# A two-block kernel on one core: every second transfer of K~ moves to SP's queue, and the fallback flag is loaded inside the order

## The chip, the cores and the metric

The kernel runs on one core of one Trainium2 chip. The metric is the device time of one execution in microseconds (us); a lower number is better. A core has five engines that run their own instruction streams: PE (TensorE, matmuls), DVE (VectorE), ACT (ScalarE), POOL (GpSimd) and SP (SyncE). PE, DVE and ACT do most of the computing; SP only issues transfers; ACT and POOL issue some too. Engines wait for each other, and for transfers, on semaphores.

## The reference

The inputs are q, k, v, a_re and a_im of shape (4, 8, 768, 48), w_in (384 x 2048) and w_out (2048 x 384), all float32. The first block is a gated linear recurrence per batch and head, the second a dense block with a squared ReLU:

```
a = (a_re + i a_im) * min(|a|, 0.999) / (|a| + 1e-6)
for t in range(768):
    S = a[t][:, None] * S + outer(k[t], v[t])     # S complex, 48 x 48
    y[t] = q[t] @ real(S)
x = y, heads side by side                         # 3072 x 384
out = relu(x @ w_in)**2 @ w_out                   # 3072 x 384
```

## The kernel before, in words

The 3072 tokens are cut into six **units** of L = 512 (n = 0 to 5, `NU` = 6). A unit has eight heads in four pairs (`NP` = 4); z = 0 and 1 are the two halves of the heads, each with two pairs (p or q_ = 0 and 1). A sequence is 768 long, so units 1 and 4 hold the end of one sequence and the beginning of the next, and units 2 and 5 hold the end of one.

For each unit, `load` brings a, q, k and v; `chain` normalises a and forms cumulative products of it (mostly DVE and ACT); `apply` inside it multiplies q and k by these products or their inverses, which gives Q~ and K~ in the tiles `ff` (the products at line 1326, K~ first). A token's place in `ff` is partition by partition with four tokens each. `gather` (line 1351) is called as soon as K~ is there: it moves K~ by DMA into `KC`, where a block i of 128 tokens (i = 0 to 3) lies on the partitions. `needs(n)` lists the blocks that are wanted: [0, 1, 2, 3] for units 0 and 3, [0, 2, 3] for 1 and 4, [0, 1, 2] for 2 and 5. `places(i)` gives one transfer for an even block and two of 64 partitions each for an odd one. In units 0 to 2 (`FINE`) a gather covers one pair (np = 1), in the later ones two.

Then come the steps of `pairs` for each pair: `turn` transposes Q~ and K~ to `QT` (DVE transposes at line 1414 and twelve transfers at line 1419, SP and ACT; some pairs by PE instead), `score` (line 1461) multiplies them, `keep` (line 1489) reads `KC` to update the state, `mix` (lines 1520 and 1524) forms y, and transfers at line 1546 (mostly SP) put y into `xT`. The dense block of the unit reads `xT`: `dense` (line 1571, then line 1619 or, for units 1 to 5, `seven` with matmuls at line 1682 in the helper `half`), and for the last unit `eleven` (line 1827) ahead of `seven`. Its outputs leave by `rows` (line 1637, POOL) or, for the last group, `side` (line 1631, SP and one by ACT). DVE's adds for it are at line 1707, its sums of activations (`put`) at line 1698.

The order of all of this isn't the order of the code. Every call of `step` or `dma` only adds an entry to a `Plan` with an engine, an estimated duration, the keys that it reads and writes, a rank and the function that issues it. `Plan.order` (line 524) is a list scheduler over the engines SP, POOL, PE, DVE and ACT: it repeatedly takes the engine that can go first and the best-ranked entry that is ready there. A transfer costs the issuing engine 0.55 us (POOL) or 0.6 us (SP, ACT), takes its turn on a common bus and lands a given time later; of POOL's transfers, and of SP's and ACT's together, at most eight are in flight. PE gets 0.3 us of margin behind another engine's result, or 1.7 us for `score` and `keep` behind a transfer, and 0.12 us for each turn between small matmuls (`score`, `mix`) and others. `Plan.emit` (line 614) then issues the functions in the planned order of their starts. So each engine's stream is in planned order, and what runs is held together by semaphores.

The fast path is valid for inputs in a certain range. `inspect` and `verdict` check that beside the last matmuls: DVE writes 0 or 1 into the one-element tile `flag` (line 1893, behind a one-column matmul at line 1891). After the fast path, `nc.values_load` (line 1958) loads the flag into a register of every engine, and `tc.If(bad > 0)` (line 1959) branches past or into `general_path`. For these inputs the branch skips the general path.

Lines 1637 (`rows`), 888 (`inspect`), 844 (`fetch`) and 949 (values v) are POOL's other transfers; lines 933 (`load`), 1419, 1546 and 1631 are SP's.

Of the kernel before, what the change touches and what calls it, by code (L numbers as in the profile page):

```python
# [481 lines left out]
class Plan:  # L482
# [5 lines left out]
    RATE = 280e3  # L488
    LANES, LANDED = 8, 0.2
    STOP, COLD = 2.4, 3.5  # L490
    TURN = 0.12
    SETTLED, GROUP = 90.0, 6
    HOLD, URGENT, FILL = {"DVE": 0.15, "ACT": 0.8}, (2, 0.2), (2, 0.2)
# [30 lines left out]
    def order(self):  # L524
# [14 lines left out]
        def small(n):  # L539
            return any(x in steps[n][3].__qualname__ for x in ("score", "mix"))  # L540
# [20 lines left out]
        while len(start) < len(steps):  # L561
# [30 lines left out]
            if e == "PE":  # L592
                if small(n) != tiled:
                    dur, tiled = dur + self.TURN, small(n)
                if t > free[e] + self.STOP:
# [15 lines left out]
        self.start, self.done = start, done  # L611
        return sorted(start, key=lambda n: (start[n], n))

    def emit(self):
        for n in self.order():
            self.steps[n][3]()


U16, I16, F16 = mybir.dt.uint16, mybir.dt.int16, mybir.dt.float16
# [3 lines left out]
def fast_path(ctx, tc, q, k, v, a_re, a_im, moe_w_in, moe_w_out, out, flag):  # L623
# [4 lines left out]
    nc = tc.nc  # L628
# [20 lines left out]
    EARLY = 2  # L649
# [12 lines left out]
    dve, pool, act, sp = nc.vector, nc.gpsimd, nc.scalar, nc.sync  # L662
# [88 lines left out]
    plan = Plan()  # L751
# [30 lines left out]
    def kk_(z, qs=(0, 1), js=range(W)):  # L782
        return [("KC", z, q_, j) for q_ in qs for j in js]

    def fk(z, *qs, ps=(0, 1)):
        return [("f", z, q_, p) for q_ in qs for p in ps]

    def dma(q, reads, writes, fn, rank, size, lat=1.8, group=None):
        name, dur = ("POOL", 0.55) if q is pool else ("SP" if q is sp else "ACT", 0.6)
        step(name, dur, reads, writes, fn, rank, (lat, size), group)  # L790
# [119 lines left out]
    def places(i):  # L910
        return [(CH, 0, CH), (0, CH, CH)] if i % 2 else [(0, 0, C)]
# [41 lines left out]
    def chain(n):  # L953
# [284 lines left out]
        def apply(z, p, np):  # L1238
# [81 lines left out]
            for j in (1, 0):  # L1320
                o = own[:, j * nh * W * R:(j + 1) * nh * W * R].rearrange(
                    "p (c h e) -> p h c e", c=W, h=nh)
                for r in range(2):
                    step("DVE", tt(n1), [("a", z), ("ap", z, p, r)] + held[r] + (kf[0] + x("kk") if j else [("qk", z)]),
                         kf[j],
                         lambda j=j, r=r, o=o: dve.tensor_tensor(  # L1326
                             out=o[:, :, :, r * D:(r + 1) * D], in0=kk if j else qk[:, 0],
                             in1=al[r], op=ALU.mult), rk)
                if j:
                    gather(n, z, p, np)  # L1330
# [11 lines left out]
    def needs(n):  # L1342

        ps_ = parts(n)
        ends = ps_[-1][3] + ps_[-1][1] * W == S
        got = [0, 1, 2] + ([] if ends else [3])
        if len(ps_) > 1:
            got.remove(1)
        return got

    def gather(n, z, p, np):
        rank = (PAIR, n)
        w = 2 * np * R
        kc = KC[z].rearrange("p (i x) -> p i x", i=W)[:, :, p * 2 * R:p * 2 * R + w]
        nat = ff[z][:, p * Z:(p + np) * Z].rearrange("p (j c x) -> p j c x", j=2, c=W)[:, 1]
        keys = fk(z, *range(2 * p + np, 2 * p + 2 * np))
        for i in needs(n):
            for p0, t0, m in places(i):
                queue = sp if n < EARLY and i % 2 else pool
                src = nat[32 * i + t0 // W:32 * i + (t0 + m) // W]  # L1360
                dma(queue, keys, kk_(z, range(p, p + np), [i]),
                    lambda i=i, p0=p0, m=m, src=src, queue=queue: queue.dma_start(  # L1362
                        out=kc[p0:p0 + m, i], in_=src),
                    rank, m * w * NEAR, GLAT, group=(n, p))
# [568 lines left out]
        inspect(i)  # L1933
    verdict()
    with tc.manual_schedule():
        plan.emit()


@with_exitstack
def kernel(  # L1940
    ctx: ExitStack,
    tc: tile.TileContext,
    q: bass.AP,
    k: bass.AP,
    v: bass.AP,
    a_re: bass.AP,
    a_im: bass.AP,
    moe_w_in: bass.AP,
    moe_w_out: bass.AP,
    out: bass.AP,  # L1950
):

    nc = tc.nc
    fp = ctx.enter_context(tc.tile_pool(name="flag", bufs=1))
    flag = fp.tile([1, 1], I32, name="flag")
    args = (q, k, v, a_re, a_im, moe_w_in, moe_w_out, out)
    fast_path(tc, *args, flag)
    bad = nc.values_load(flag[0:1, 0:1], min_val=0, max_val=1)
    with tc.If(bad > 0):
        general_path(tc, *args)  # L1960

# [29 lines left out]
```

## Time and profile before

| | |
|---|---|
| median of three runs | 663.11 us (662.74 to 663.75) |
| the profiled execution | 663.12 us |
| its span, first to last instruction | 661.2 us |
| mean granted clock of TensorE | 0.990 |
| DMA packets, bytes | 55268, 80.35 MB |

The profile is one execution, recorded on the chip. Its page gives the busy time of each engine, the span in 40 slices (16.5 us each; a digit is the busy share in tenths), the chain of work that ended last, and the costliest groups of instructions by source line. Further views can be asked of the trace: who waited for whom, the stretches with each engine's busy time, the instructions of one line, the timeline of one engine. PEld is the loading of weights into PE. A letter q behind an engine (SPq, ACTq) means its sequencer: an instruction that issues, waits or branches. An issue of a DMA shows only the time to issue it; the landing is listed apart. A duration written as three numbers is least, median and most in ns.

### The profile page before, as it was taken

To read this page: it belongs to the slowest core of one execution; us is meant where nothing else is said; L and a number is where in the kernel's file an instruction comes from. 1 tells how busy PE (TensorE), PEld (TensorE's weight loads), DVE (VectorE), ACT (ScalarE), POOL (GpSimd) and SP (SyncE) were. 2 spreads that over 40 slices of the span, in tenths; PEclk is the share of its full clock that TensorE was granted. 3 is DMA by queue.
4 is the path that set the end of the run, shared out by engine and by line. 5 is a ranking of instruction groups with operands and counts; after the bars stand their busy time and mean duration, and the time that the engine had idled before them with its cause. 6 is when DMAs were issued, how large, how long until landed. Compare 5 with 4: busy or idle time off the path is not lost.

```text
span 661.2 us, 12107 instructions
## 1 busy us (share of the span) xinstructions
PE 620.8 (94%) x4454; PEld 555.5 (84%) x4454; DVE 583.9 (88%) x1191; ACT 347.0 (52%) x606; POOL 118.7 (18%) x198
## 2 busy tenths in 40 slices
PE   0378999999999999999999999999999999999996
PEld 0357887687779988999989989989999989988996
DVE  7999999898998999998989888998879989559971
ACT  7748979985746345348263357363366352045300
POOL 7401040401100032040121040111040111032200
PEclk9979999999999999999999999999999999999999
DMA  7953686305530055570056571046470054367730
GB/s 227 313 224 79 150 208 187 70 3 153 143 89 1 7 133 143 134 185 1 12 128 165 133 159 30 14 117 169 121 181 0 25 121 89 92 202 262 250 113 27
DMA packets 55268, 80.35 MB, mean 122 GB/s; under 512 B 11392, under 2 KB 37920, under 8 KB 55200
## 3 DMA queue, kind: packets, MB, share of 16 engines
q0 software_dynamic: 15424, 42.12, 22.5%
q1 hardware_dynamic: 35168, 31.93, 19.0%
q10 hardware_dynamic: 4608, 5.44, 3.2%
q8 instruction: 37, 0.61, 0.4%
q14 instruction: 31, 0.25, 0.1%
HBM read 48.76 MB, written 4.72 MB: 81 GB/s over the span
## 4 chain that ended last, share of the span: by engine, by line
PE 89%; DVE 7%; ACT 2%; issue 1%; DMA 1%; SPq 0%; DVEq 0%; ACTq 0%
PE d L1571 29%; PE d L1682 28%; PE d L1619 6%; PE sc L1461 5%; PE tr L1489 4%; PE yp L1520 3%; PE yp L1524 2%; PE d L1827 2%; PE tr L1827 2%; PE sc L1571 2%; PE sc L1827 1%; PE tr L1060 1%; DVE f L1261 1%; PE d L1440 1%; PE tr L1440 1%; PE yp L1571 1%
## 5 line engine op out<-in xcount | busy, mean ns | idle before, releaser
L1571 PE MATMUL d<-xT,w 128*128 128x256 f32 x888 | 198.5, 380 | 0.0
L1571 PEld LDWEIGHTS d<-xT,w 128*128 128x128 f32 x888 | 166.9, 190 | 23.1 <-issue 0.6
L1682 PE MATMUL d<-T,g 128*128 128x192 f32 x576 | 98.7, 327 | 0.0
L1682 PEld LDWEIGHTS d<-T,g 128*128 128x128 f32 x576 | 93.6, 190 | 0.3
L1604 ACT ACTIVATE g<-d 128x512 f32<-128x512 f32 x74 | 44.1, 596 | 83.6 <-PE d L1571 68.3
L1682 PE MATMUL d<-w,g 128*128 128x192 f32 x432 | 76.1, 329 | 0.0
L1637 POOL DMA_DIRECT2D out_dram<-ot x40 | 25.6, 644 | 277.6 <-DVE ot L1707 223.3
L1682 PEld LDWEIGHTS d<-w,g 128*128 128x128 f32 x432 | 70.4, 190 | 1.6 <-issue 0.7
L1362 POOL DMA_DIRECT2D KC<-f x60 | 32.4, 558 | 141.1 <-DVE f L1326 99.1
L1698 DVE TENSOR_TENSOR g<-g 128x512 f32<-128x512 f32 x72 | 48.5, 689 | 8.7 <-ACT g L1605 4.5
L1605 ACT ACTIVATE g<-g 128x512 f32<-128x512 f32 x80 | 50.5, 631 | 2.6
L1261 DVE TENSOR_TENSOR f<-aq,xn 128x384 f32<-128x384 f32 (+1 forms) x72 | 46.8, 687 | 0.0
L1619 PE MATMUL d<-w,g 128*128 128x384 f32 x128 | 44.0, 490 | 0.0
L1414 DVE STREAM_TRANSPOSE aq<-f 128x384 f32<-128x384 f32 (+1 forms) x51 | 42.7, 912 | 0.2
L1026 DVE TENSOR_TENSOR f<-aq 128x384 f32<-128x384 f32 x72 | 37.2, 554 | 0.8
L1461 PEld LDWEIGHTS sc<-QT 96*64 96x64 f32 x736 | 33.5, 137 | 3.6 <-issue 2.8
L1461 PE MATMUL sc<-QT 96*64 96x128 f32 (+1 forms) x736 | 36.0, 249 | 0.2 <-ACT QT L1444 0.2
L1619 PEld LDWEIGHTS d<-w,g 128*128 128x128 f32 x128 | 23.5, 190 | 13.7 <-issue 0.2
L1707 DVE TENSOR_TENSOR ot<-ot,d 128x192 f32<-128x192 f32 x70 | 23.7, 350 | 12.5 <-PE d L1682 12.0
L1464 DVE TENSOR_TENSOR A<-sc,mask 128x512 f32<-128x512 f32 x45 | 29.9, 685 | 3.2 <-PE sc L1461 3.1
L1533 ACT COPY yt<-yp 112x512 f32<-112x512 f32 (+1 forms) x20 | 11.6, 579 | 37.2 <-PE yp L1524 37.1
L1292 ACT ACTIVATE f<-aq 128x768 f32<-128x768 f32 (+1 forms) x16 | 17.3, 1082 | 24.7 <-DVE aq L1278 24.6
(279 smaller groups left out, 1119.5 us busy)
## 6 DMA issues: line engine op xcount, KB each, us to landing
QT<-aq SPq DMA_DIRECT2D x136, 64.0 KB, 2.0
f<-in_moe_w_in_dram POOLq DMA_DIRECT2D x8, 768.0 KB, 6.9
f<-in_moe_w_out_dram POOLq DMA_DIRECT2D x8, 768.0 KB, 5.1
QT<-aq ACTq DMA_DIRECT2D x68, 64.0 KB, 2.1
KC<-f POOLq DMA_DIRECT2D x40, 96.0 KB, 3.4
out_dram<-ot POOLq DMA_DIRECT2D x40, 96.0 KB, 3.7
xT<-yt SPq DMA_DIRECT2D x34, 96.0 KB, 2.4
T<-in_moe_w_out_dram POOLq DMA_DIRECT2D x4, 768.0 KB, 9.9
```

The source lines that it names most:

```text
L1026: lambda c=c, j=j: dve.tensor_tensor(out=f[:, j], in0=a[:, :, :, c - 1], in1=a[:, j, :, c].unsqueeze(1).to_broadcast([C, 2, HH, D]), op=AL ...
L1261: lambda j=j, r=r: dve.tensor_tensor(out=f4[:, j, r], in0=a[:, r], in1=over(j), op=ALU.mult), rk)
L1362: lambda i=i, p0=p0, m=m, src=src, queue=queue: queue.dma_start(out=kc[p0:p0 + m, i], in_=src),
L1414: lambda src=src, dst=dst: dve.transpose(out=dst, in_=src), rank)
L1461: pe.matmul(sa[p0:p0 + CH, j, t0:], lhsT=T[:, j, 1, h, t0:t0 + CH], rhs=T[:, j, 0, h, t0:], start=True, stop=True)
L1571: pe.matmul(ps, lhsT=w1[:, f // FP, m, ts(f % FP, C)], rhs=xT[:, n % 2, m, ts(grp, G)], start=(m == 0), stop=(m == NM - 1))
L1604: act.activation(out=o, in_=ps, func=AF.Relu)
L1605: act.activation(out=o, in_=o, func=AF.Square)
L1619: pe.matmul(ps, lhsT=gt[:, f % 2, ts(i, C)], rhs=w2[:, f], start=(f == 0), stop=(f == NF - 1))
L1682: pe.matmul(bank[b][:, 0:DH], lhsT=gsets[x][h][:, j - HW * h, r], rhs=w(j), start=first and j == 0, stop=last and j == NT - 1)
L1698: lambda: dve.tensor_tensor(out=g[:, :, o], in0=g[:, :, x0], in1=g[:, :, x1], op=op),
L1827: pe.matmul(ps[:, jj], lhsT=u[:, ts(jj, C)], rhs=v_, start=i == 0, stop=i == len(terms) - 1)
```

## The change

Two things are edited. In `gather`, the transfers of the odd blocks i were issued by SP only for the first two units (`EARLY` = 2) and by POOL after that; now they are SP's for every unit. The even blocks stay with POOL. The planner sees the new engine too, as it does for every transfer.

And `Plan.emit` takes a function `ask`: ahead of the first entry whose planned start lies less than `ASKED` = 12.0 us before the latest planned start, it calls it. `fast_path` passes the load of the flag, and returns the register value to the kernel's body, where the load stood behind the fast path. The branch stays where it was.

```diff
@@ class Plan
     STOP, COLD = 2.4, 3.5
+    ASKED = 12.0
     TURN = 0.12
@@
-    def emit(self):
-        for n in self.order():
+    def emit(self, ask):
+        order = self.order()
+        end = max(self.start.values())
+        asked = None
+        for n in order:
+            if asked is None and self.start[n] > end - self.ASKED:
+                asked = ask()
             self.steps[n][3]()
+        return asked
@@ gather
-                queue = sp if n < EARLY and i % 2 else pool
+                queue = sp if i % 2 else pool
@@ fast_path
     with tc.manual_schedule():
-        plan.emit()
+        return plan.emit(lambda: nc.values_load(flag[0:1, 0:1], min_val=0, max_val=1))
@@ tile_gateloop__then__act_relu_squared_kernel
-    fast_path(tc, *args, flag)
-    bad = nc.values_load(flag[0:1, 0:1], min_val=0, max_val=1)
+    bad = fast_path(tc, *args, flag)
     with tc.If(bad > 0):
         general_path(tc, *args)
```

## The prediction

> **What bounds the kernel now.** I read the page from the top: busy shares, the 40 slices, the chain that ended last.
>
> ```profile
> PE 620.8 (94%) x4454; PEld 555.5 (84%) x4454; DVE 583.9 (88%) x1191; ACT 347.0 (52%) x606; POOL 118.7 (18%) x198
> PE   0378999999999999999999999999999999999996
> PE 89%; DVE 7%; ACT 2%; issue 1%; DMA 1%; SPq 0%; DVEq 0%; ACTq 0%
> ```
>
> TensorE is the bound from the fourth slice on, and the chain runs through it for 89% of the span. A busy PE isn't proof of a PE that never waits, so the next views are the stretches, and then the waits of PE and of its weight loads after the ramp.
>
> ```profile
> 220.00:340.00 120.00, 120.00 (x853) 111.34 (x852) 114.12 (x236) 56.91 (x103) 24.06 (x40) 1.00 0.38 95
> 340.00:460.00 120.00, 120.00 (x946) 111.39 (x946) 106.98 (x202) 59.05 (x105) 17.19 (x28) 1.00 0.48 114
> 460.00:580.00 120.00, 120.00 (x958) 111.89 (x954) 100.72 (x196) 49.16 (x83) 15.83 (x25) 1.00 0.37 91
> 580.00:655.60 75.60, 75.60 (x416) 70.37 (x412) 56.82 (x106) 23.05 (x39) 14.02 (x19) 1.00 0.55 182
> PE tr L1060 <- DVE xn L1188: 0.2, 1, 0.2
> PEld yp L1520 <- issue: 3.5, 13, 0.5
> ```
>
> The columns of the stretches are PE, PEld, DVE, ACT and POOL busy, then the granted clock, the DMA share and GB/s. PE is busy for all 435.6 us from 220 to 655.6, at a full clock. The last two rows are the longest of PE's waits after 100 us and of PEld's after 170 us: 0.2 us in one piece, and 3.5 us in 13 pieces that no DMA and no engine ended. So between the ramp and the last matmul there is no wait for K~, or for anything else, that could be taken away. What is left on the path is the tail behind the last matmul.
>
> **The tail, and the flag.** After the last add on DVE comes the last output transfer (ACT), then on each engine the flag's load and the branch, then the closing barriers.
>
> ```profile
> 655.69 0.35 DVE L1707 TENSOR_TENSOR ot<-ot,d 128x192 f32<-128x192 f32 x1 [2.25 <-PE d L1682]
> 656.08 0.38 ACTq L1631 DMA_DIRECT2D out_dram<-ot  x1
> L1958 SPq TENSOR_LOAD <-flag x1: 471/471/471, 640.6 to 640.6; - x1
> L1958 PEldq TENSOR_LOAD <-flag x1: 492/492/492, 652.6 to 652.6; - x1
> L1958 DVEq TENSOR_LOAD <-flag x1: 535/535/535, 655.7 to 655.7; - x1
> L1958 ACTq TENSOR_LOAD <-flag x1: 480/480/480, 656.5 to 656.5; - x1
> L1959 ACTq COMPARE_BRANCH  x1: 58/58/58, 657.0 to 657.0; - x1
> L1959 ACTq EVENT_SEMAPHORE  x1: 17/17/17, 660.2 to 660.2; - x1
> SPq L1986 <- ACTq L1959: 0.4, 1, 0.4
> ```
>
> Read it as two branches that meet. ACT issues its transfer at 656.08 to 656.46, loads the flag at 656.5 (0.48 us), branches at 657.0, and shows its next instruction only at 660.2, 3.2 us after the branch. SP meanwhile waits for the landing of that transfer and walks through its closing semaphores. The last row says who is late: SP waits 0.4 us for ACT. With the load out of ACT's tail, its branch moves from 657.0 to about 656.5 and its next instruction from 660.2 to 659.7, 0.5 us earlier. But after 0.4 us of that SP's own sequence is the last, so **the gain is 0.4 us**, bounded by 0 (if the landing slips) and by 0.55 (the load with its gaps). What is late next is the landing and SP's walk behind it. DVE's load (at 655.7, under the add) and PE's (at 652.6) leave the tail too, but neither was last. SP's and POOL's loads stood at 640.6 already.
>
> The Trainium skill, "DMA: Bandwidth & Descriptors", section "Latency and other measured facts", gives a register load from memory a floor of about 0.6 us. By that figure ACT's tail would shrink by 0.6 and not by 0.5; the cap of 0.4 us holds either way, and the measured 0.48 us decides here.
>
> **The load inside the order.** It is emitted ahead of the first step that the plan starts within 12.0 us of its last start. The last start on the trace is ACT's transfer at 656.08, so that place is near 644.1. This part adds waits: each engine's queue stands still until the flag is there and for half a microsecond more. The flag's rows and what lies around them:
>
> ```profile
> 639.67 0.19 PE L1891 MATMUL tr<-col,good 128*1 128x1 f32 x2
> 640.38 0.14 DVE L1893 TENSOR_SCALAR flag<-tr 1x1 int32<-1x1 f32 x1
> 645.29 0.69 DVE L1698 TENSOR_TENSOR aq<-aq 128x512 f32<-128x512 f32 x1 [0.61 <-PE d L1682]
> 652.89 2.76 PE L1682 MATMUL d<-T,aq 128*128 128x192 f32 x16
> ```
>
> On PE the matmuls of `half` are queued behind the load, and everything else waits for those. Its queue was at the load at 652.6 while 16 matmuls, the last of which ends at 655.65, were still ahead: it runs about 2.9 us ahead of the array. At a place near 644.1 it arrives near 641.2, finds the flag (written by 640.52), and is through by 641.7, with some 2.4 us of matmuls in hand. Cost 0; with that cover gone, 0.49 us. On DVE a put of line 1698 stands behind it, like the one at 645.29, before which DVE idles 0.61 us for PE; the load's 0.535 us fits into such a gap. On ACT and SP only output transfers of `side` are left, which wait for later adds, and POOL's last step is behind it. **Sum of this part: 0.** It is bounded by 0 and by 1.2 us, worked out below as a rival.
>
> **The K~ transfers.** For the units n = 2 to 5 the blocks i = 1 and 3 go to SP, two transfers each. By `needs` that is i = 1 in n = 2, both in n = 3, i = 3 in n = 4 and i = 1 in n = 5; n = 2 has four gathers of half width, the others two. So 8 transfers of 48 KB, and 8, 4 and 4 of 96 KB, 24 in all, leave POOL.
>
> ```profile
> KC<-f POOLq DMA_DIRECT2D x40, 96.0 KB, 3.4
> KC<-f POOLq DMA_DIRECT2D x8, 48.0 KB, 2.2
> KC<-f SPq DMA_DIRECT2D x24, 48.0 KB, 2.9
> L1362 POOL DMA_DIRECT2D KC<-f x60: 512/550/602, 54.0 to 553.8; - x60
> L1362 SPq DMA_DIRECT2D KC<-f x24: 544/592/1085, 53.7 to 168.3; - x24
> 231.10 2.17 POOL L1362 DMA_DIRECT2D KC<-f  x4 [0.96 <-PE d L1682]
> 238.43 1.14 PE L1489 MATMUL tr<-v,KC 128*96 128x48 f32 x12
> 333.76 3.21 POOL L1362 DMA_DIRECT2D KC<-f  x6 [2.56 <-issue]
> 342.67 1.48 PE L1489 MATMUL tr<-v,KC 128*96 128x48 f32 x16
> ```
>
> The eight of 48 KB are n = 2's. Issuing costs 0.59 us on SP against 0.55 on POOL, so the move takes 24 x 0.55 = 13.2 us from POOL and puts 24 x 0.59 = 14.2 us on SP, in parallel. A group of 4 issues (2.17 us) becomes two and two, one of 6 (3.21 us) two and four: the last issue comes 1.1 us (2 x 0.55) or about 0.9 us (3.21 less 4 x 0.59) earlier. Landing, for 48 KB, takes 2.9 us from SP against 2.2 from POOL, though SP's rows lie in the busier first units; I take the 0.7 us as the worst case, and 1.1 as the best. Neither reaches PE: in n = 2 the last of the four issues starts at 232.72 (231.10 + 2.17 - 0.55) and lands near 234.9, and `keep` reads it from 238.43, 3.5 us later. In n = 3 it is 336.42 + 3.4 = 339.8 against 342.67, 2.8 us. PE works on dense matmuls in between. POOL is 18% busy and nobody waits for its queue. **Cost and gain on the path: 0.** What hides it are the dense matmuls that fill PE; with that cover gone it would be -1.1 to +0.7 us for each group.
>
> The Trainium skill, "Advanced Engine Details and Errata", section "DGE: Hardware vs Software", puts the first byte at about 0.6 us on the hardware path against 1 us on POOL's software path. By that page K~ would land 0.4 us earlier from SP, where the rows of 48 KB show it 0.7 us later; no run here shows yet the two on the same unit, and with 2.8 us in hand the sum is 0 by either.
>
> **What the planner does with it.** The order is written by a list scheduler that knows these costs, so from the first K~ of n = 2 (231 us) the order itself can change; before that it can't. PE's work stays the same; its turns between small and dense matmuls don't.
>
> ```profile
> 244.51 3.95 PE d L1571 x18
> 248.46 1.49 PE sc L1461 x32
> 249.95 2.79 PE d L1571 x12
> 254.63 1.34 PE sc L1461 x32
> 288.35 9.06 PE d L1571 x42
> ```
>
> Scores after dense work take 1.49 us, right after other small work 1.34: 0.15 us to turn. Twelve dense matmuls after small ones take 2.79 us, by the rate of the 42 (9.06 / 42 = 0.216) they would take 2.59: 0.20 to turn back. One excursion more or less is 0.35 us. I take no net change, with one excursion either way.
>
> **Sum**: -0.4 (tail) + 0 + 0 + 0. The profiled execution took 663.12 us (span 661.2 and 1.9 around it), which is the median of the runs, 663.11. So 662.7.
>
> **The rivals.**
> *Forecast, same, 662.7* (own range 662.0 to 663.6: an excursion of 0.35 either way, the tail between 0 and 0.55). Chance 0.65. About 0.2%, 1.3 us, is what a measurement of this kernel can tell from no change.
> *Fewer turns.* With K~ planned about 1 us earlier, keeps and scores bunch better, and three or more excursions fall away: 663.1 - 3 x 0.35 - 0.4 gives 661.7, faster. For it: PE's stalls are gone, and turns are all that is left to win between 231 us and the tail. Against: the planner groups small work already, and nothing says that the new order groups better. Chance 0.13.
> *SP becomes the queue that is late: slower.* SP issues the QT transfers in long runs:
>
> ```profile
> 337.60 10.80 SPq L1419 DMA_DIRECT2D QT<-aq  x16
> 348.50 1.35 SPq L933 DMA_DIRECT2D aq<-in_a_re_dram  x2
> 578.79 0.43 PE L1520 MATMUL yp<-A,v 128*48 128x128 f32 x4
> 580.68 1.13 PE L1827 MATMUL sc<-xT,w 128*128 128x256 f32 x4
> ```
>
> Sixteen issues take 10.8 us without a pause, and the scores of a pair wait for the last of its own. If the K~ issues (four in n = 3, 4 x 0.59 = 2.4 us, two elsewhere, 1.2 us) wait for DVE at the head of SP, or get in among the QT, the scores come that much later. It decides where PE's dense filler ends before the late scores: by n = 5 it just lasts, since the last small run at 578.79 is followed at once by the next stage at 580.68. The price is 2.4 us in n = 3 alone, 663.1 - 0.4 + 2.4 = 665.1 with the tail won, and up to 6.0 us (1.2 + 2.4 + 1.2 + 1.2) over the four units. Against it: K~ is ready before the transposes that feed QT, and in n = 3 POOL has issued all of it by 336.97 (333.76 + 3.21), before SP's run of QT starts at 337.60. Chance 0.17.
> *The flag's load stalls PE.* If the order puts it right behind the flag's own matmul (639.67 to 639.86), PE has nothing queued until the load ends, 640.52 + 0.5 = 641.0: 1.2 us, so 663.9, within the bound of same. It decides at a place ahead of 641.0, 3 us before the one I expect. Chance 0.05.
> *The change doesn't do what it says*, in that the tail's end is the landing and not ACT: 663.1. This lies in the forecast's own range.
>
> **How the numbers follow.** Faster by over 0.2%: 0.13. Within: 0.65 + 0.05 = 0.70. Slower: 0.17. The range goes from 661.3 (four turns fewer) to 665.1 (n = 3's price), which leaves out the larger halves of the two outer cases, under 0.2.
>
> **What would show it.** Right: no flag load on ACT after the last transfer, ACT's branch at its end, the first instruction behind it 0.5 us sooner relative to the last add, and SP's wait for ACT gone. PE still fully busy from 220 us to its last matmul, at the same length to within an excursion. K~ rows of SP 48, of POOL 36, and keeps still microseconds behind the landing. Wrong: PE waits of DMA on QT or KC, a gap of PE near 641 to 645, or a last matmul more than a microsecond off 655.65.

## The result and the profile after

The changed kernel takes 670.86 us (median of four runs, 669.28 to 672.41) against 663.43 us (four runs, 662.74 to 664.39). The ratio is 1.01, with a 95% interval of 1.0079 to 1.0122: **slower by 7.4 us**. The profiled execution took 672.3 us, with a span of 670.0 us. Lines of the changed kernel are higher by 7 (by 6 in the closing part): 1571 is now 1578, 1682 is 1689. The load of the flag is on line 1943.

The page of the changed kernel first: busy shares, PE in the 40 slices, the shares of the chain.

```profile
PE 625.2 (93%) x4454; PEld 558.8 (83%) x4454; DVE 581.9 (87%) x1191; ACT 347.1 (52%) x606; POOL 106.1 (16%) x174
PE   0478999999999999999999979999999999999996
PE 84%; DVE 11%; DMA 1%; ACT 1%; issue 1%; SPq 0%; DVEq 0%; ACTq 0%
```

PE has the same 4454 matmuls. One slice of the settled part, the 24th (385.3 to 402.0 us), fell from 9 to 7. The stretches resolve it (columns as in the prediction), first of the changed kernel, then the kernel before at the same place:

```profile
220.00:340.00 120.00, 120.00 (x854) 111.56 (x854) 111.89 (x234) 60.41 (x108) 17.78 (x28) 1.00 0.36 88
385.00:390.00 5.00, 4.24 (x42) 3.50 (x39) 4.71 (x10) 3.11 (x6) 2.75 (x4) 1.00 0.46 123
390.00:395.00 5.00, 0.77 (x4) 0.34 (x2) 3.63 (x4) 1.90 (x4) 1.78 (x3) 0.85 1.00 193
395.00:400.00 5.00, 4.97 (x12) 3.97 (x13) 4.83 (x11) 1.15 (x2) 0.00 (x0) 0.50 1.11 224
400.00:405.00 5.00, 5.00 (x24) 4.36 (x23) 1.14 (x4) 2.53 (x5) 0.00 (x0) 0.97 0.23 49
```

```profile
390.00:395.00 5.00, 5.00 (x25) 4.41 (x24) 4.83 (x11) 3.19 (x6) 2.10 (x3) 1.00 1.11 195
395.00:400.00 5.00, 5.00 (x28) 4.43 (x27) 2.72 (x11) 3.83 (x10) 0.00 (x0) 1.00 0.96 173
```

From 385 to 395 us PE stands still for 5.0 us, and from 395 to 400 us it does 12 matmuls at a granted clock of 0.50, where the kernel before did 25 of the same shape in 5 us at a full clock (390 to 395 us; the 28 of the next row include six smaller ones). From 220 us to the last matmul it is as full as before everywhere else. PE's two longest waits after 100 us, and PE's timeline there, of the changed kernel:

```profile
PE d L1578 <- DMA xT<-yt: 4.3, 1, 4.3
PE yp L1527 <- DVE A L1471: 0.6, 1, 0.6
```

```profile
383.59 1.51 PE L1468 MATMUL sc<-QT 96*64 96x128 f32 x32
385.74 1.03 PE L1527 MATMUL yp<-A,v 128*48 128x128 f32 x7 [0.64 <-DVE A L1471]
...
387.91 2.86 PE L1578 MATMUL d<-xT,w 128*128 128x256 f32 x12
395.03 9.33 PE L1578 MATMUL d<-xT,w 128*128 128x256 f32 x30 [4.26 <-DMA xT<-yt]
```

The same place in the kernel before, the end of the same unit 3:

```profile
377.65 1.51 PE L1461 MATMUL sc<-QT 96*64 96x128 f32 x32
...
381.94 0.39 PE L1524 MATMUL yp<-QT,St 96*48 96x128 f32 x4
382.26 1.57 PE L1682 MATMUL d<-w,g 128*128 128x192 f32 x8
383.66 2.76 PE L1682 MATMUL d<-T,g 128*128 128x192 f32 x16
386.26 10.52 PE L1571 MATMUL d<-xT,w 128*128 128x256 f32 x48
```

The last scores of the unit come 5.9 us later in the changed kernel (383.59 against 377.65). What matters next is the filler: dense matmuls that are ready, and that PE can do while y goes through the transfers into xT. Before, PE had 24 matmuls of line 1682 after its last `mix`, and the first 12 of the 48 of line 1571, which don't read the last rows of xT: an estimate from these rows is 6.6 us (12 x 10.52 / 48 = 2.6, so to 388.9 from 382.3). In the changed kernel only those 12 (2.86 us) are left, and between the last scores and the last `mix` there is nothing at all. Then PE waits 4.26 us for xT. What xT comes through is seen in the issues from 383 us on, with KB each and the median time to landing, changed kernel and then before:

```profile
aq<-in_q_dram SPq DMA_DIRECT2D x4, 192.0 KB, 8.0
v<-in_v_dram POOLq DMA_DIRECT2D x4, 96.0 KB, 5.8
xT<-yt SPq DMA_DIRECT2D x3, 96.0 KB, 5.4
```

```profile
xT<-yt SPq DMA_DIRECT2D x2, 96.0 KB, 3.4
```

The last rows of xT land in 5.4 us instead of 3.4, among unit 4's loads of v and q. Before, SP had issued xT by 384.1 us, ahead of all these loads; in the changed kernel it issues it from 384.4 to 390.1 us, while POOL issues six loads of v from 387.3 us.

**The accounting** of the profiled execution, by the last add on DVE (655.69 before, 664.64 after, 8.95 us later): 0.76 us idle from 385 to 390 us, 4.26 us for xT, and the half clock. That began at 393.5 us (0.85 in the stretch from 390) and ended at 400.3 us (0.97 in the stretch from 400); 5.3 us of it fell on work, which costs 2.65 us. With 0.71 us by which PE was later already at 231 us (the dense matmuls that start at 230.66 before start at 231.37 after), up to where the two orders are the same, that is 8.38 of 8.95 us. The remaining 0.57 us isn't followed up.

**The tail** behaved in part as forecast. Of the changed kernel, the closing rows and SP's waits, and then SP's wait before:

```profile
L1943 ACTq TENSOR_LOAD <-flag x1: 478/478/478, 649.5 to 649.5; - x1
L1965 ACTq COMPARE_BRANCH  x1: 58/58/58, 665.4 to 665.4; - x1
L1965 ACTq EVENT_SEMAPHORE  x1: 17/17/17, 668.9 to 668.9; - x1
SPq L1965 <- SPq L1965: 5.0, 2, 2.7
```

```profile
SPq L1959 <- SPq L1959: 4.8, 2, 2.5
```

ACT loads the flag 15 us before its last transfer and branches 0.8 us after the start of the last add, 1.3 us before. SP's wait for ACT is gone. But ACT's next instruction comes 3.5 us behind its branch, where it was 3.2, so that it is only 0.25 us sooner relative to the last add and not 0.5. And SP's longest wait among its closing semaphores, read here as that for the last landing, is 0.2 us longer. From the last add to the end it is 5.36 us against 5.51.

### The profile page after: what moved, and what is told of

The parts are those of the page before. It is cut to its first block, busy times and chain, and to the rows that moved or that the text cites. A ratio compares the mean times of both kernels' runs of the same rounds, so it can differ in the third digit from the quotient of the medians.

```text
span 670.0 us, 12091 instructions
## 1 busy us (share of the span) xinstructions
PE 625.2 (93%) x4454; PEld 558.8 (83%) x4454; DVE 581.9 (87%) x1191; ACT 347.1 (52%) x606; POOL 106.1 (16%) x174
## 4 chain that ended last, share of the span: by engine, by line
PE 84%; DVE 11%; DMA 1%; ACT 1%; issue 1%; SPq 0%; DVEq 0%; ACTq 0%
PE d L1578 29%; PE d L1689 27%; PE d L1626 6%; PE sc L1468 4%; PE tr L1496 3%; PE yp L1527 3%; PE yp L1531 2%; PE d L1834 2%; PE tr L1834 2%; PE sc L1578 2%; PE sc L1834 1%; DVE f L1333 1%; DVE f L1268 1%; PE tr L1067 1%; DVE f L1033 1%
## 5 line engine op out<-in xcount | busy, mean ns | idle before, releaser
L1578 PE MATMUL d<-xT,w 128*128 128x256 f32 x888 | 200.9, 384 | 4.3 <-DMA xT<-yt 4.3
L1578 PEld LDWEIGHTS d<-xT,w 128*128 128x128 f32 x888 | 168.8, 192 | 28.4 <-issue 5.2
L1369 POOL DMA_DIRECT2D KC<-f x36 | 20.1, 563 | 147.0 <-DVE f L1333 105.6
```

The source lines that it names most:

```text
L1578: pe.matmul(ps, lhsT=w1[:, f // FP, m, ts(f % FP, C)], rhs=xT[:, n % 2, m, ts(grp, G)], start=(m == 0), stop=(m == NM - 1))
```

## The experiments

Every kernel is compared with runs of the kernel before on the same chip (medians 663.60 us for e1 to e4, 663.79 for e5 to e8 and 663.84 for e9 and e10), so kernels of different chips are best compared by their ratios. "Order" means the plan's. PE's longest wait is that of the profiled execution after 100 us. The traces of e1, e2, e4 and e5 show no gap of PE over 0.6 us, close to what was expected of them, but their times were forecast too low: they lie 0.7 to 1.7 us above the upper ends of the expected ranges. e6, too, is 1.9 us above its own.

| | us | ratio, 95% interval | PE's longest wait |
|---|---|---|---|
| e1 flag alone | 664.01 | 1.0002 (0.9993 to 1.0011) | 0.3 |
| e10 transfers alone | 672.10 | 1.0091 (1.0060 to 1.0121) | 5.0 for xT |
| e2 SP issues, order of before | 665.19 | 1.0023 (1.0010 to 1.0035) | 0.6 |
| e3 POOL issues, new order | 670.48 | 1.0103 (1.0069 to 1.0136) | 4.6 for xT |
| e4 all but unit 2 | 663.99 | 1.0007 (0.9998 to 1.0017) | under 0.2 |
| e8 unit 2 alone | 670.99 | 1.0116 (1.0099 to 1.0132) | 3.5 for xT |
| e5 QT first in unit 2 | 664.90 | 1.0036 (1.0017 to 1.0054) | 0.2 |
| e9 mix not held back | 664.74 | 1.0010 (1.0000 to 1.0021) | 0.2 |
| e6 PE kept warm | 669.94 | 1.0101 (1.0080 to 1.0122) | 0.6 |
| e7 v behind xT | 667.16 | 1.0051 (1.0036 to 1.0065) | 1.8 for xT |

### Which part: e1 and e10

e1 keeps the flag's load inside the order and takes back the transfers; e10 does the opposite.

```diff
# e1
-                queue = sp if i % 2 else pool
+                queue = sp if n < EARLY and i % 2 else pool
# e10
-        return plan.emit(lambda: nc.values_load(flag[0:1, 0:1], min_val=0, max_val=1))
+        plan.emit()
...
+    bad = nc.values_load(flag[0:1, 0:1], min_val=0, max_val=1)
```

> Before, with the flag's load inside the order and K~ issued as before. Theory (the planner's new order is what costs): nothing of the 7.4 us stands here; PE busy from 220 us to its last matmul, and the tail shorter by 0.2 to 0.4 us, so 663.0 to 663.2 against 663.4. Rival (the load stalls an engine in the order): a gap on PE between 639 and 646 us and a time above 664.

> The K~ transfers moved as in the change, the flag loaded at the end as before. Theory (the load inside the order is worth nothing either way): 670 to 672 us, like the full change. Rival (the load inside the order costs or gains something beside the new order): more than 1.5 us away from the full change, below 669 or above 673.

The flag alone is the kernel before to within 0.1%. Its median shows no gain in the tail, and PE has no gap from 639 to 646 us, where the rival put a stall. The transfers alone give the whole loss (672.10 against 670.86 us, intervals over each other), with the same wait:

```profile
PE d L1572 <- DMA xT<-yt: 5.5, 2, 5.0
```

### Queue or order: e2 and e3

The planner is told one engine and the code issues on another. In e2 the planner counts the moved transfers as POOL's, so that the order stays that of e1, and SP issues them. In e3 the planner counts them as SP's, and POOL issues them.

```diff
# e2
+                planned = sp if n < EARLY and i % 2 else pool
-                dma(queue, keys, kk_(z, range(p, p + np), [i]),
+                dma(planned, keys, kk_(z, range(p, p + np), [i]),
# e3
-                queue = sp if i % 2 else pool
+                queue = sp if n < EARLY and i % 2 else pool
+                planned = sp if i % 2 else pool
-                dma(queue, keys, kk_(z, range(p, p + np), [i]),
+                dma(planned, keys, kk_(z, range(p, p + np), [i]),
```

> The changed kernel, but the planner counts the moved transfers as POOL's: they are issued by SP, and every engine's order is that of before. Theory (order): no gap on PE, 663 to 663.5. Rival (SP's queue: 24 more issues there make QT, xT and the loads of the next unit late): most of the loss is here too, 668 or more, with PE waiting for QT or xT.

> The opposite: the planner counts the transfers as SP's and writes the changed kernel's order, but POOL issues them as before. Theory (order): 669 to 672, with the same wait for xT near 390 us and the half clock behind it. Rival (SP's queue): back to 663 to 664.

e3, with no K~ transfer moved on the chip, has the loss and the picture of the full change; its wait, and a stretch behind it at half clock:

```profile
PE d L1579 <- DMA xT<-yt: 4.6, 1, 4.6
```

```profile
395.20:398.20 3.00, 3.00 (x9) 2.34 (x8) 2.90 (x7) 0.00 (x0) 0.00 (x0) 0.50 1.12 226
```

So **the order is what costs, not the queue**. The queue probably costs something too: e2 is 1.2 us slower than e1 by the medians (665.19 against 664.01; the intervals just touch), with two new waits that e1 doesn't have,

```profile
PE yp L1528 <- DVE A L1472: 0.6, 1, 0.6
PE d L1579 <- DVE ot L1715: 0.4, 1, 0.4
```

the first near 577 us, in unit 5. There SP's run of QT starts 2.2 us later than in e1 (562.94 against 560.75), and 1.3 of these were lost ahead of the first moved transfer. The rest fits the rival of SP's late queue, with a cost by the medians of half its price for n = 3 and a fifth of its highest one, but no run separates it further.

### Which unit: e4 and e8

```diff
# e4
+                queue = sp if n != 2 and i % 2 else pool
# e8
+                queue = sp if n < 3 and i % 2 else pool
```

> The changed kernel with unit 2 taken out: K~ of odd blocks by SP in units 0, 1, 3, 4 and 5. Theory (the order goes wrong from unit 2 on, where the first different steps stand): no gap on PE, 662.7 to 663.3, although unit 3 has the most transfers moved. Rival (unit 3's own four issues per half hold up its QT): a wait for xT near 390 us as in the changed kernel, 667 or more.

> Of the units behind the first two only unit 2 is moved to SP (8 transfers of 48 KB). Theory (unit 2 alone turns the order): slower than before although only a third of the transfers is moved, 666 or more, with PE waiting somewhere behind 380 us. Rival (the loss grows with the transfers on SP): within 1 us of before.

Sixteen of the 24 moved transfers (units 3 to 5) cost nothing that can be measured. The eight of unit 2 alone, 48 KB each, cost as much as all 24. In e8 the wait falls one unit later, near 487 us, though the last moved transfer is issued some 230 us ahead of it (256.6 us); the wait, and the stretch in which it ends and the half clock begins:

```profile
PE d L1578 <- DMA xT<-yt: 4.0, 2, 3.5
```

```profile
489.00:494.00 5.00, 3.27 (x8) 2.67 (x9) 4.79 (x5) 0.44 (x1) 0.43 (x1) 0.67 1.10 238
```

### Which decision of the planner: e5 and e9

In unit 2 the two orders part like this. PE from the first scores to the second pair's, before and after:

```profile
248.39 1.56 PE L1461 MATMUL sc<-QT 96*64 96x128 f32 x32
249.88 2.86 PE L1571 MATMUL d<-xT,w 128*128 128x256 f32 x12
252.67 0.43 PE L1520 MATMUL yp<-A,v 128*48 128x128 f32 x4
...
254.47 1.50 PE L1461 MATMUL sc<-QT 96*64 96x128 f32 x32
```

```profile
249.09 1.56 PE L1468 MATMUL sc<-QT 96*64 96x128 f32 x32
250.58 5.45 PE L1578 MATMUL d<-xT,w 128*128 128x256 f32 x24
255.87 1.46 PE L1689 MATMUL d<-w,g 128*128 128x192 f32 x8
257.26 0.43 PE L1527 MATMUL yp<-A,v 128*48 128x128 f32 x4
...
259.06 1.51 PE L1468 MATMUL sc<-QT 96*64 96x128 f32 x32
```

From the first scores to the first `mix` it was 4.28 us with 12 dense matmuls; it is 8.17 us with 32. PE is busy in both, which is why the stretch from 220 to 340 us shows nothing: 20 dense matmuls of filler are spent early, and the pairs behind come later. ACT's issue of one of the second pair's QT transfers shows the other side, before and after:

```profile
246.54 0.52 ACTq L1419 DMA_DIRECT2D QT<-aq  x1
```

```profile
250.33 0.52 ACTq L1426 DMA_DIRECT2D QT<-aq  x1
```

It is 3.8 us later, behind other ACT work, so the second pair's scores are planned later. And `Plan.order` has a rule that groups small steps: where PE isn't in small work and another small step becomes ready within `GROUP` = 6 us, it takes a dense one first. With the scores planned later, but within 6 us, it holds the first `mix` back for longer. By the planner's own times it is held once in the order before, at 251.0 us, for scores that are ready at 252.2, and three times in the changed order, at 252.3, 253.6 and 254.9 us, for scores ready at 255.1. e5 ranks ACT's QT transfers of unit 2 first; e9 leaves them late and switches that rule off from 250 to 257 us of planned time, where this `mix` is the only step that it holds.

```diff
# e5
-                            in_=T6[32 * b:32 * b + 32, i % 2, j]), rank, 16384 * NEAR, TLAT,
+                            in_=T6[32 * b:32 * b + 32, i % 2, j]), (-1, n) if queue is act and n == 2 else rank, 16384 * NEAR, TLAT,
# e9
-                if small(n) and not tiled and any(
+                if small(n) and not tiled and not 250 < t < 257 and any(
```

> The changed kernel in full, with one rank altered: in unit 2 the transfers of QT that ACT issues come ahead of its other work in the planner. Theory (in the new order one of these is passed by other work on ACT, the second pair's scores of unit 2 come late, the first pair's mix is held back to go with them, and PE spends its dense filler early): no gap near 390 us, 662.7 to 663.5. Rival (K~ on SP in units 2 and 3 makes the pairs late whatever ACT does): the gap stays, 667 or more.

> The full change, but the list scheduler's rule that holds a small step back while another becomes ready within 6 us is off between 250 and 257 us of planned time, where it holds back the first mix of unit 2. Theory (that one held mix is what makes PE spend its dense filler early): the mix stands about 252 us again, PE has no wait for xT near 390 and no half clock, and the time is 663.5 to 665.5 us, with the moved issues of SP worth about a microsecond at most. Rival (the loss comes from later steps of the new order, or from K~ landing late): a PE wait of 3 us or more in unit 3 or 4 stays, 668 us or more.

e9 has SP's moved transfers, the late QT transfer and everything else of the change. Its PE in unit 2, and ACT's issue:

```profile
249.20 1.56 PE L1468 MATMUL sc<-QT 96*64 96x128 f32 x32
250.69 2.86 PE L1578 MATMUL d<-xT,w 128*128 128x256 f32 x12
253.48 0.43 PE L1527 MATMUL yp<-A,v 128*48 128x128 f32 x4
```

```profile
250.40 0.51 ACTq L1426 DMA_DIRECT2D QT<-aq  x1
```

The `mix` stands 4.28 us behind the first scores again, with 12 dense matmuls between, PE has no wait over 0.2 us after 100 us, and the time is 664.74 us. **One held `mix` at 253 us is worth about 6 of the 7.4 us** (670.86 - 664.74 = 6.1; by the ratios, 1.0100 against 1.0010, 0.9%). What is left, 0 to 0.2% by the interval, is of the size of e2's. e5 shows the same from the cause's side: with the transfer early the `mix` is held no longer than before, PE has no gap near 390 us, and in the profiled execution the last add stands at 655.78 us, 0.09 behind that of before. Its 1.8 us in the profile are a wait of SP for ACT at the very end. Nine of its twelve runs lie between 664.4 and 665.5 us and three between 667.0 and 670.5; why those three are slower stays open, since one execution alone is profiled.

How four gathers on SP came to put that QT transfer behind other ACT work was followed only in the plan, not by a run of its own. Nor is the way from 253 us to the gap followed step by step: e9 shows that the one leads to the other, and unit 3's last scores show it on the way (377.65 us before, 383.59 in the changed kernel, 380.21 in e9).

### What the gap costs: e6 and e7

e6 puts 16 matmuls on `ident`, into a spare bank, in front of the dense step that waits; their results aren't used. In the trace they are 32 records and take 3.73 us. e7 holds unit 4's loads of v back until the last rows of xT have landed.

```diff
# e6
-        def part_of(f, ps, ms):
+        def part_of(f, ps, ms, idle=0):
             def go():
+                for _ in range(idle):
+                    pe.matmul(bank["tr0"][:, 0:C], lhsT=ident, rhs=ident, start=True, stop=True)
...
+                cold = n == 3 and grp == 0 and late and f2 == 0
...
-                     part_of(f, ps[:, j], (NM - 1,) if late else range(NM)), rank)
+                     part_of(f, ps[:, j], (NM - 1,) if late else range(NM), 16 * cold), rank)
# e7
+            if n == 4 and i == 0:
+                step("POOL", 0.2, xk(n - 1, [NM - 1]), [("gate", 4)], lambda: pool.tensor_copy(
+                    out=gate[:, 2:3], in_=xT[:, (n - 1) % 2, NM - 1, L - 1:L]), vrank)
-                dma(pool, [("gate", 2)] if n == 2 else xk(n - (vs(n) == vs(n - 1)), [NM - 1])
+                dma(pool, [("gate", n)] if n in (2, 4) else xk(n - (vs(n) == vs(n - 1)), [NM - 1])
```

> The changed kernel with 16 extra matmuls on constants put on PE where it waits for xT near 390 us (they write a spare bank that nothing reads afterwards). The wait for the landing stays, but PE is idle for under 1.5 us. Theory (part of the loss is the halved clock behind the wait, 5.3 us of work at half speed, 2.7 us): 668 or a little less, the granted clock at 1.0 from 390 to 405 us, and no second group of times 3 us higher. Rival (the wait alone makes the whole loss): no change from the changed kernel.

> The changed kernel with the loads of v for unit 4 made to wait on POOL until the last rows of unit 3's xT have landed. Theory (the landing of these rows, 5.6 us against a median of 2.5, is late because six loads of v were issued just ahead of it): landing within 3.5 us, PE's wait near 390 us down from 4.3 us to about 2, no half clock or a shorter one, 665 to 668. Rival (the loads of q and k behind them in SP's queue, or the write itself, make it late): landing stays above 5 us, 669 or more.

The stretches of e6, with the clock full where it was 0.85 and 0.50:

```profile
390.00:395.00 5.00, 5.00 (x39) 4.73 (x38) 3.43 (x4) 2.08 (x4) 1.98 (x3) 1.00 0.98 195
395.00:400.00 5.00, 5.00 (x25) 4.38 (x24) 4.83 (x10) 2.48 (x5) 0.00 (x0) 1.00 1.12 216
```

The clock is settled by it: with PE kept busy it isn't halved, and 25 matmuls go through where 12 did. The time isn't: the profiled execution is 3.3 us below that of the full change (668.98 against 672.30), but the median of 669.94 us only 0.9, with nearly the same ratio (1.0101 against 1.0100), where the half clock had been reckoned at 2.65. So e6 is inconclusive on what the half clock is worth in the median. The extra matmuls may cost something themselves, since they take their 3.73 us also in a run in which xT lands sooner; that isn't shown. e7's wait for xT:

```profile
PE d L1581 <- DMA xT<-yt: 1.8, 1, 1.8
```

The wait falls from 4.3 to 1.8 us, the slowest of the five xT transfers lands in 3.4 us instead of 5.7, the clock stays at 1.00, and the time falls by 3.7 us to 667.16 us, clear of the full change's interval. So the loads of v share in the late landing, but what starts the loss is that PE has no filler there.

No version beat the kernel before. e4, with 16 transfers moved, equals it.

## Why the prediction was wrong, step by step

- **What bounds the kernel: right, but read too narrowly.** PE was full at a full clock, and nothing could be won between the ramp and the tail. What the stretches don't show is how much filler PE has in hand at each place; the filler ahead of xT near 386 us, 6.6 us of it before and 2.86 after, was the reserve that went.
- **The tail, -0.4: right in its mechanism, not in its sum.** ACT's load left, its branch came 0.5 us earlier, SP's wait for ACT went. But from the last add to the end of the span, which is 5.51 us before, the profiled executions with the load moved show no steady gain: 5.36 in the changed kernel, 5.69 in e1, 5.73 in e4. In e9, where SP waits 2.5 us at the longest as before, it is 5.05, 0.46 less. Where it is longer, SP's wait is too (2.7 us in e1, 2.8 in e4), as with a landing that slips. The median of e1 shows no gain; the lower bound of 0 holds.
- **The load inside the order, 0: right.** In e1 PE's load stood at 643.2 us, and PE was busy for all of the 7 us from 639 to 646.
- **The K~ transfers, 0 on the path: right for units 3 to 5** (e4), and for the transfers of unit 2 as such, since in e9 they are on SP too and only 0 to 0.2% is left. Issues moved as counted:

```profile
L1369 SPq DMA_DIRECT2D KC<-f x48: 544/594/1692, 54.4 to 561.8; - x48
L1369 POOL DMA_DIRECT2D KC<-f x36: 536/556/602, 54.7 to 562.0; - x36
```

- **The step that failed is "What the planner does with it": "I take no net change, with one excursion either way".** It priced a new order by turns between small and dense work, 0.35 us each. The new order has the same work and PE is as full up to 385 us, but it spends the filler in another place. The step put the loss of filler ahead of a later wait at nothing, without a reason. It cost about 6 us (e9), 17 times its bound: a wait of 4.26 us for xT, with the half clock behind it.
- **The rival "SP becomes the queue that is late"** had the point from which it decides, "where PE's dense filler ends before the late scores", and it gave unit 3 a price of its own. But its cause isn't what lost the 7.4 us: SP's queue alone is worth about 1.2 us (e2 against e1), and the loss is there without it (e3). So that "slower" came out isn't to this rival's credit. And its price was that of the delay alone. When the filler ended, a landing among another unit's loads and a half clock came on top.
- **What would show it wrong** named waits on QT and KC, and a last matmul more than a microsecond off 655.65. The second sign came: it ended at 664.60. But the wait came on xT, a transfer that the change doesn't touch.

## What to carry to other kernels

Where an order is written by a planner, an edit to one transfer's engine is an edit to everything behind it: compare the two orders, and look for the places where the bound engine has least in hand, before pricing the edit by its own instructions. A busy engine shows no loss while it spends work that was meant to cover a later wait; count the filler between two dependent steps in both traces. To separate order from queue, let the planner count one engine and issue on the other.

## What the runs showed of the hardware

**Half clock after a short gap.** In the changed kernel PE's last matmul ended at 390.8 us, and the clock was halved from 393.5 to 400.3 us, 6.8 us long; in e3 the gap began at 390.2 us and the half clock lasted from 395.1 to 398.5 us, 3.4 us long, all of it on work. In e10 it came 2.4 us after PE went idle and lasted 6.8 us, in e8 3.4 us after and lasted 3.4 us. A gap of 1.8 us (e7) left the clock at 1.00. So it came 2.4 to 4.9 us after PE went idle (in e3 0.3 us after PE had work again) and lasted 3.4 us or twice that. The Trainium skill, "TensorE: Matmul & The Clock Gate", section "What's actually happening", describes a free-running activity window of about 3.4 us after whose idle the clock is halved: the lengths agree, and the halving after 2.4 us (e10) and 2.7 us is sooner than a whole idle window. An estimate from these rows, half of the half-clock time that fell on work, is that a gap of 3.5 to 5 us in PE cost 1.7 (e3) to 2.65 us beside its length; no median shows it (e6). The runs of the changed kernel lie near 669.3 and near 672.4 us. The half clock alone doesn't explain these 3.1 us, and since only one of the four is profiled, they stay open.

**The same K~ transfers on both queues.** The two transfers of 48 KB issued between 230 and 234.5 us in unit 2, from POOL before and from SP after:

```profile
KC<-f POOLq DMA_DIRECT2D x2, 48.0 KB, 2.2
```

```profile
KC<-f SPq DMA_DIRECT2D x2, 48.0 KB, 3.0
```

On the same unit SP's land 0.8 us later (0.7 in e9, 0.8 in e5), close to the prediction's worst case for this part, 0.7. These are two transfers in each trace, beside others in flight. The Trainium skill, "Advanced Engine Details and Errata", section "DGE: Hardware vs Software", puts the first byte 0.4 us earlier on SP's hardware path; the landings here don't show that gain. What else differs is the number of packets: by the two pages, the same 1.97 MB of all moved transfers left POOL's queue as 1024 packets and came to SP's as 1920. Whether that is what makes them later isn't shown.
